# A fused attention and expert kernel: scores tied behind matmul groups, maxima in other PSUM banks, a new ration of groups a step

## The chip, the cores and the metric

The kernel runs on one core of one Trainium2 chip. The metric is the device time of one execution in microseconds (us). TensorE does the matmuls, VectorE (DVE), ScalarE (ACT) and GpSimd (POOL) the elementwise work, and SyncE (SP) issues nearly all DMAs.

## The reference

Attention with rotary positions over 4 batches, 8 heads, 576 positions and head size 64, then two expert layers on the 2304 tokens, all in f32:

```python
scores = scale * np.matmul(q_rot, k_rot.transpose(0, 1, 3, 2))
attn = np.exp(scores - np.max(scores, axis=-1, keepdims=True))
attn = attn / (np.sum(attn, axis=-1, keepdims=True) + 1e-09)
attn_out = np.matmul(attn, v)
...
x = attn_out.transpose(0, 2, 1, 3).reshape(B * S, H * D)      # 2304 x 512
h = np.maximum(np.maximum(x @ w1, x @ w2), x @ w3)            # d_ff 768
x = h @ w_out
h = x @ w_in                                                  # d_ff 2048
out = (h * (1.0 / (1.0 + np.exp(-h)))) @ w_out2
```

## The kernel before

**Tiles and steps.** Heads are taken in pairs (`hp`, 4 a batch), and a batch's 576 query rows in two parts: 256 rows (tiles 0 and 1) and 320 rows (tiles 2, 3 and 4, the last of 64 rows). That makes 80 tiles; `attention()` runs one step `j` for each and five steps more. In step j it traces the scores of tile j (`tile_scores`: one small product for the last keys, then two of 512 columns, one for each head, on 64 rows of the array each), their maximum on VectorE (`tile_max`, L436) and two Exps on ScalarE (L443); behind these come, for the tile of the step before, the division by the sum (`tile_norm`, L452 to L455) and four SP copies that move blocks of e to pt (`tile_move`, L494); for the tile two steps back, the last key column's transpose (`tile_last`, L505, L461); and for the tile three steps back the flip (`tile_flip`, L516), a transpose of 32 x 32 blocks on VectorE. When a part of a head pair is complete, `av` multiplies it with v (L557, then eight products of 64 output columns, L561) and splits the result into two f16 halves x (L564 on ScalarE, L565 on VectorE). That is the way of batches 1 to 3 (`moved(b)`); batch 0 turns all its blocks on TensorE (`tile_turn`). `qk_turn` transposes a pair's q and k (L373, L387) one pair ahead. `av_at` and `x_ready` say in which step a part's value product is traced and from which step its x may be used.

**Groups.** The first expert layer (`moe1`) is a generator of matmul groups, of which each fills one PSUM bank (L649): 12 matmuls of 256 or 320 columns for w1, w2, w3, and 18 for w_out. A group's result is emptied by ScalarE (L665) or VectorE (L667). Two banks, ring `ps_m` with the tag m, are there for groups while attention runs. After each step the main loop traces groups by a ration: `debt` grows by `RATE = 8000` columns, and each group takes off its own. A part's groups may start once `x_ready` is reached.

**PSUM.** A tile's scores take three banks and there is one such tile (`ps_s`); two banks (`ps_t`, tag tr) hold turned pieces and last columns; one (`ps_x`) the value product; two (m) the groups and, through `max_bank`, the maxima over all partitions that set the f16 scales (`all_max_a` transposes, VectorE reduces, `all_max_b` spreads; L120 and L128 on TensorE). When attention is over, its six banks are given back and five more hold groups (mg).

**Side work.** Beside all this the second layer's weights are loaded, narrowed to f16 halves and combined: L227 on ScalarE, L229 on GpSimd, L238 and L239 on VectorE (`narrow_b`), L153 on ScalarE, L917, L921 and L925 for the combinations, and about six SP transfers a step. `tc.issue_after(last["max"])` puts some of these behind the step's maximum on VectorE.

**Order.** Each engine's instructions stand in one fixed queue. A scheduler in the build makes that order from the traced program, with its own idea of durations; `with tc.issue_after(x):` forces an instruction behind x on its engine. A matmul of a later group may therefore stand ahead of, behind or between the score products of a tile.

Of the kernel before, what the change touches and what calls it, by code (L numbers as in the profile page):

```python
# [7 lines left out]
F32 = mybir.dt.float32  # L8
# [9 lines left out]
P = 128  # L18
# [4 lines left out]
def fused_kernel(  # L23
# [22 lines left out]
    nc = tc.nc  # L46
    B, H, S, D = q.shape
    NP = H // 2
# [60 lines left out]
    zscr = {nm: dram.tile([P, KC * (F2 // 512) * 512], F32, name="z" + nm) for nm in ("wi", "wo")}  # L109


    ps_am = []

    def max_bank():
        return (ps_am[0] if ps_am else ps_m).tile([P, 512], F32, tag="m", name="m")

    def all_max_a(m, ps=None):

# [240 lines left out]
    def moved(b):  # L359
        return b > 0  # L360
# [219 lines left out]
    for b, hp, r in order:  # L580
        first.setdefault((b, hp), len(tiles))
        tiles += [(b, hp, t) for t in PARTS[r][2]]
        av_at.setdefault(len(tiles) + 2 + moved(b), []).append((b, hp, r))
        x_ready[b, r] = len(tiles) + 4 + moved(b)
    for i, (b, hp) in enumerate(pairs):
        u = first[b, hp]
        if b > 1:
# [11 lines left out]
    for b in range(1, B):  # L599
# [4 lines left out]
        at(u, v_scale, b)  # L604
        at(u + 1, v_scale_b, b)

    def attention():

        back = lambda j, n: tiles[j - n] if n <= j < len(tiles) + n else None
        for j in range(len(tiles) + 5):  # L610
            if j < len(tiles):
                tile_scores(tiles[j])
                tile_max(tiles[j])
            key = back(j, 3)
            if key and moved(key[0]):
                tile_flip(key)
            for a in av_at.pop(j, ()):
                av(*a)
            key = back(j, 1)
            if key:  # L620
                tile_norm(key)
                if moved(key[0]):
                    tile_move(key)
            key = back(j, 2)
            if key:
                (tile_last if moved(key[0]) else tile_turn)(key)
            for f, a in events.pop(j, ()):
                f(*a)
            yield
# [11 lines left out]
    def group(passes, n, ps=None, more=False):  # L641

        first = ps is None
        if first:
            wide_n[0] += 1
            ring, tag = (ps_g[0], "mg") if ps_g and wide_n[0] % 7 > 1 else (ps_m, "m")
            ps = ring.tile([P, 512], F32, tag=tag, name=tag)
        for i, (l, r) in enumerate(passes):
            nc.tensor.matmul(ps[:, 0:n], l, r, start=(first and i == 0), stop=(not more and i == len(passes) - 1))  # L649
        return ps  # L650

    def moe1(b, pools):
# [632 lines left out]


    RATE = 8000
    debt = 0
    next(wprep)
    moe = wprep2 = None  # L1290
# [9 lines left out]
    for j, _ in enumerate(attention(), 1):  # L1300
        if moe is None:
            for _ in range(1 + (j > 7)):
                next(wprep, None)
            if j >= x_ready[0, 0]:
                for _ in wprep:
                    pass
                wprep2 = prep_wo1(stage2)
                moe = moe_groups()
                nxt = next(moe)
            continue  # L1310
        next(wprep2, None)
        if x_p.get(1) is not None:
            for _ in range(1 + (j % 4 == 0) if j > 20 else 0):
                next(wprep3, None)
            if hasattr(WI, "s"):
                wprep4 = wprep4 or prep_w8(1.7)
                next(wprep4, None)
        debt = min(debt + RATE, 3 * RATE)
        while debt > 0 and nxt[0] < B - 1 and j >= x_ready[nxt[0], nxt[1]]:
            debt -= nxt[2]  # L1320
            nxt = next(moe)
        if nxt[0] == B - 1 and j > len(tiles) - 4 and nxt[1] == 0:
            nxt = next(moe)
    for _ in wprep3:
        pass
    for _ in wprep4:
        pass
    attn_pools.close()
    tail = ExitStack()
    ps_g.append(Ring(tail, "ps_g", 5, space=PSUM))  # L1330
# [82 lines left out]
```

## Time and profile before

| what | value |
| --- | --- |
| time, median of 3 runs | 1001.32 us (1000.82 to 1008.92) |
| profiled execution | 1006.66 us, span 1004.8 us |
| mean granted TensorE clock | 0.969 |
| busy share PE, DVE, ACT, POOL | 92%, 70%, 60%, 49% |

The profile is of one execution, which is slower than the median of the runs. A clock of 1.0 is 2.4 GHz, 0.5 is 1.2 GHz. Shares are averages over stages with different limits: up to about 590 us attention and the first expert layer run together, to about 660 us the rest of the first expert layer, and then the second expert layer.

### The profile page before, as it was taken

How to read it: one execution, taken by the hardware profiler on the slowest of the kernel's cores; microseconds unless marked ns; L12 is line 12 of the kernel's file. 1: busy time of each engine (PE TensorE's matmuls, PEld its weight loads, DVE VectorE, ACT ScalarE, POOL GpSimd, SP SyncE). 2: the span in 40 equal slices, each digit the busy share in tenths (PEclk: the TensorE clock that was granted, in tenths of full speed). 3: DMA queues.
4: the chain of work that ended last, by engine and by line, in shares of the span. 5: the costliest groups of instructions: out<-in, count | busy, mean ns of one | idle time of the engine just before them, and what ended most of it. 6: DMA issues, size and time to landing. Idle time of an engine off the chain costs nothing. (4 is left out here: it accounts for less than half of the span.)

```text
span 1004.8 us, 19162 instructions
## 1 busy us (share of the span) xinstructions
PE 922.8 (92%) x6802; PEld 674.3 (67%) x6802; DVE 698.6 (70%) x1231; ACT 604.4 (60%) x1381; POOL 490.9 (49%) x546
## 2 busy tenths in 40 slices
PE   4577999999999899998998989999998999999997
PEld 2344665555666556665655567788887888888886
DVE  5779877967578556897767546854778767856554
ACT  2888577757667656787867623653563544554442
POOL 5835594961455500633322205653678259255264
PEclk9798999999999899999998999999999999999999
DMA  6943135877788965789988846264454253333201
GB/s 150 295 118 104 34 100 120 190 143 161 165 180 191 183 107 96 203 225 228 215 212 188 205 115 212 72 189 147 134 188 132 74 174 102 114 122 125 66 1 42
DMA packets 185198, 146.29 MB, mean 146 GB/s; under 512 B 51216, under 2 KB 168720, under 8 KB 185104
## 3 DMA queue, kind: packets, MB, share of 16 engines
q1 hardware_dynamic: 183600, 144.36, 56.5%
q8 instruction: 54, 0.88, 0.4%
q10 hardware_dynamic: 1504, 0.72, 0.3%
q14 instruction: 40, 0.33, 0.1%
HBM read 90.51 MB, written 26.21 MB: 116 GB/s over the span
## 5 line engine op out<-in xcount | busy, mean ns | idle before, releaser
L649 PEld LDWEIGHTS <-w 128*128 128x128 f16 x1632 | 161.5, 100 | 70.7 <-issue 24.5
L649 PE MATMUL m<-x,w 128*128 128x256 f16 (+1 forms) x1388 | 195.4, 292 | 13.1 <-ACT t L665 6.0
L1139 PEld LDWEIGHTS <-g 128*128 128x128 f16 x1485 | 146.2, 98 | 17.6
L1076 PEld LDWEIGHTS <-w8s 128*128 128x128 f16 x1344 | 131.1, 98 | 16.1 <-issue 1.0
L436 DVE TENSOR_REDUCE nb<-s 128x2 f32<-128x1152 f32 (+1 forms) x80 | 98.7, 1233 | 42.0 <-PE s L426 38.1
L443 ACT ACTIVATE e<-s,nb 128x576 f32<-128x576 f32 x144 | 105.3, 737 | 35.2 <-DVE nb L436 33.0
L917 POOL TENSOR_TENSOR z<-z 128x128 f32<-128x128 f32 (+1 forms) x96 | 60.8, 652 | 127.7 <-DMA z<-zwi 49.4
L229 POOL TENSOR_SCALAR z<-z 128x256 uint16<-128x256 uint16 x64 | 52.9, 826 | 123.0 <-ACT z L227 77.7
L455 ACT ACTIVATE e<-e,rec 128x576 f32<-128x576 f32 x144 | 104.5, 768 | 12.9 <-DVE rec L453 12.4
L426 PE MATMUL s<-T 64*128 64x512 f32 x256 | 85.9, 707 | 0.0
L561 PE MATMUL xp<-pt,vd 128*64 128x256 f32 (+1 forms) x512 | 81.5, 416 | 2.7 <-DVE pt L516 2.7
L1090 POOL TENSOR_TENSOR z<-t 128x256 f32<-128x256 f32 x32 | 27.1, 847 | 89.0 <-DVE t L1082 54.0
L516 DVE STREAM_TRANSPOSE pt<-pt 128x1024 f32<-128x1024 f32 (+1 forms) x60 | 67.6, 1127 | 2.8 <-DMA pt<-e 2.8
L1028 DVE SCALAR_TENSOR_TENSOR g<-gsum,sg,g 128x1024 f16<-128x1024 f32 x36 | 49.1, 1372 | 23.5 <-ACT g L1027 23.1
L352 POOL TENSOR_TENSOR w<-qk,sin_sb 128x512 f32<-128x512 f32 (+2 forms) x44 | 45.0, 1044 | 40.7 <-DMA qk<-in_q_dram 37.5
L649 PE MATMUL m<-h,wo 128*128 128x256 f16 (+1 forms) x448 | 63.2, 291 | 0.0
L1027 ACT ACTIVATE g<-gsum,sg 128x1024 f16<-128x1024 f32 x36 | 40.9, 1143 | 36.5 <-POOL gsum L1023 36.5
L649 PEld LDWEIGHTS <-wo 128*128 128x128 f16 x512 | 50.3, 100 | 17.2 <-issue 2.7
L561 PEld LDWEIGHTS xp<-pt,vd 128*64 128x64 f32 x512 | 35.9, 136 | 37.6 <-issue 13.4
L239 DVE SCALAR_TENSOR_TENSOR z<-z,z 128x256 int32<-128x256 int32 x64 | 36.3, 567 | 20.2 <-POOL z L229 19.0
L667 DVE SCALAR_TENSOR_TENSOR t<-m,t 128x256 f32<-128x256 f32 (+1 forms) x82 | 36.8, 449 | 18.5 <-PE m L649 15.7
L1139 PE MATMUL c<-w,g 128*128 128x256 f16 x376 | 48.9, 277 | 0.0
(246 smaller groups left out, 1970.7 us busy)
## 6 DMA issues: line engine op xcount, KB each, us to landing
w8s<-w8scr SPq DMA_DIRECT2D x64, 448.0 KB, 4.4
pt<-e SPq DMA_DIRECT2D x192, 128.0 KB, 4.0
z<-in_moe_w_in_dram SPq DMA_DIRECT2D x32, 256.0 KB, 3.9
z<-in_moe_w_out_dram SPq DMA_DIRECT2D x32, 256.0 KB, 3.7
w<-in_moe_w_dram SPq DMA_DIRECT2D x6, 768.0 KB, 5.2
wo<-in_moe_w_dram SPq DMA_DIRECT2D x6, 768.0 KB, 4.6
qk<-in_q_dram SPq DMA_DIRECT2D x32, 128.0 KB, 3.2
vd<-in_v_dram SPq DMA_DIRECT2D x16, 256.0 KB, 3.1
```

The lines of the kernel that those rows point to most:

```text
L229: nc.gpsimd.tensor_scalar(out=q[:, :, 2], in0=q[:, :, 1], scalar1=step, scalar2=off, op0=ALU.mult, op1=ALU.add)
L426: last["s"] = last["score"] = nc.tensor.matmul(s[:, o:o + 512], qs[r], kt[r], start=True, stop=True).ins
L436: x = nc.vector.tensor_reduce(out=nb[:, 0:m], in_=both(s, 0, 960, 576) if m > 1 else s[:, 0:576], op=ALU.max, axis=AX.X, negate=True)
L443: x = nc.scalar.activation(out=e[:, HK[g]], in_=s[:, SK[g]], func=AF.Exp, bias=nb[:, g:g + 1], accum_out=sm[:, g:g + 1])
L455: nc.scalar.activation(out=e[:, HK[g]], in_=e[:, HK[g]], func=AF.Copy, scale=r[:, g:g + 1])
L516: nc.vector.transpose(out=x, in_=x)
L561: nc.tensor.matmul(xp[r, 0:n], v4[:, g, c, :], turned(c, g), start=False, stop=(c == 3))
L649: nc.tensor.matmul(ps[:, 0:n], l, r, start=(first and i == 0), stop=(not more and i == len(passes) - 1))
L917: nc.gpsimd.tensor_tensor(out=z[:, o], in0=z[:, x], in1=z[:, y], op=op)
L1028: nc.vector.scalar_tensor_tensor(out=l, in0=x, scalar=sg_t[jb], in1=h, op0=ALU.mult, op1=ALU.subtract)
L1076: nc.tensor.matmul(o, l, r, start=(i == 0), stop=(i == len(passes) - 1))
L1139: x = nc.tensor.matmul(ps, l, r, start=first, stop=last_, skip_group_check=True)
```

## The change

Four things change. First, `max_bank` takes its bank from the turns' ring (tr) while the step's number is over `LOOSE = 25` and attention runs. Second, from the 27th tile on `tile_scores` stands inside `tc.issue_after(last["group"])`: a tile's scores come behind the last group that was traced before them. Third, for the last batch's second part, `tile_flip` comes two steps behind the tile instead of three, and `av` and `x_ready` come one step earlier. Fourth, from that tile on the ration of a step is `pace[j - 1]`: 13600 columns, less 3650 for the scores, 5800 for each value product and 2900 for each `qk_turn` of the step.

```diff
     def max_bank():
-        return (ps_am[0] if ps_am else ps_m).tile([P, 512], F32, tag="m", name="m")
+        ring, tag = (ps_am[0], "m") if ps_am else (ps_t, "tr") if b_now[0] else (ps_m, "m")
+        return ring.tile([P, 512], F32, tag=tag, name=tag)
...
-        av_at.setdefault(len(tiles) + 2 + moved(b), []).append((b, hp, r))
-        x_ready[b, r] = len(tiles) + 4 + moved(b)
+        lag = int(moved(b) and (b, r) != (B - 1, 1))
+        av_at.setdefault(len(tiles) + 2 + lag, []).append((b, hp, r))
+        x_ready[b, r] = len(tiles) + 4 + lag
...
+    LOOSE = 25
+    LAST = [(B - 1, hp, t) for hp in range(NP) for t in PARTS[1][2]]
+
     def attention():
...
+            b_now[0] = int(j > LOOSE)
             if j < len(tiles):
-                tile_scores(tiles[j])
+                with tc.issue_after(last["group"]) if j > LOOSE else nullcontext():
+                    tile_scores(tiles[j])
                 tile_max(tiles[j])
-            key = back(j, 3)
-            if key and moved(key[0]):
-                tile_flip(key)
+            for n in (3, 2):
+                key = back(j, n)
+                if key and moved(key[0]) and n == 3 - (key in LAST):
+                    tile_flip(key)
...
-            nc.tensor.matmul(ps[:, 0:n], l, r, start=(first and i == 0), stop=(not more and i == len(passes) - 1))
+            x = nc.tensor.matmul(ps[:, 0:n], l, r, start=(first and i == 0), stop=(not more and i == len(passes) - 1))
+        last["group"] = x.ins
...
+    costs = {av: 5800, qk_turn: 2900}
+    pace = [13600 - 3650 - sum(costs[f] for f, _ in jobs) for jobs in (
+        [(av, a) for a in av_at.get(j, ())] + [x for x in events.get(j, ()) if x[0] is qk_turn] for j in range(len(tiles) + 5)
+    )]
...
-        debt = min(debt + RATE, 3 * RATE)
+        debt = min(debt + (pace[j - 1] if j > LOOSE else RATE), 3 * RATE)
```

The lines of the kernel after are numbered 1 to 9 higher than those of the kernel before. On TensorE, at the 28th tile, before: the tile's scores (bank set s) with their second large product behind four groups; the "..." stands for the matmuls of four groups in banks m 1, m 0.

```order
L561 MATMUL xp_0_2236<-pt_1_1889,vd5_0_131 64x256 x8
L423 MATMUL s_0_2225<-kd3_0_125,T_3_1897 128x2x64
L426 MATMUL s_0_2225<-T_3_1897 128x512
L649 LDWEIGHTS w1_0_138
L649 MATMUL m_1_1994<-x_0_457,w1_0_138 128x320
...
L426 MATMUL s_0_2225<-T_3_1897 128x512
L505 MATMUL tr_1_2258<-ident_0_78,e_1_2081 128x128
L649 LDWEIGHTS w1f_0_137
L649 MATMUL m_1_2060<-x_0_457,w1f_0_137 128x320
```

And the same tile after:

```order
L657 MATMUL m_1_2210<-x_0_457,w1_0_138 128x320
L424 MATMUL s_0_2225<-kd3_0_125,T_3_1897 128x2x64
L427 MATMUL s_0_2225<-T_3_1897 128x512 x2
L506 MATMUL tr_1_2258<-ident_0_78,e_1_2081 128x128
L657 LDWEIGHTS w1_0_138
L657 MATMUL m_0_2281<-x_0_457,w1_0_138 128x320
```

The two large products now stand together, behind the last matmul of the group in m_1_2210, which was four groups later in the old order.

On TensorE, in the drain behind the 80th tile's scores, before: the end of one group in bank m 0 (m_0_6674), a value product (xp), and the start of the next group, again in bank m 0 (m_0_6704).

```order
L649 MATMUL m_0_6674<-x_0_5504,w1_0_138 128x256
L557 MATMUL xp_0_6646<-pt_0_6326,vd2_0_128 128x320
L505 MATMUL tr_0_6666<-ident_0_78,e_0_6544 128x128
L561 MATMUL xp_0_6646<-pt_0_6326,vd2_0_128 64x320 x8
L649 LDWEIGHTS w1_0_138
L649 MATMUL m_0_6704<-x_0_5504,w1_0_138 128x256
```

And after:

```order
L558 MATMUL xp_0_6487<-pt_0_6176,vd2_0_128 128x320
L562 MATMUL xp_0_6487<-pt_0_6176,vd2_0_128 64x320 x8
L657 LDWEIGHTS w1_0_138
L657 MATMUL m_0_6678<-x_0_5350,w1_0_138 128x256
...
L506 MATMUL tr_0_6553<-ident_0_78,e_0_6409 128x128
...
L657 MATMUL m_1_6693<-x_0_5350,w1_0_138 128x256
```

The value product comes ahead of the groups, and these alternate between the two banks m.

On VectorE, at the maximum of the 71st tile (nb), before: one flip (of tile 68) behind it, then narrowing (z), a combination (z8, w8o), evacuations (h1, t) and a reciprocal (rec), up to the 72nd tile's maximum.

```order
L436 TENSOR_REDUCE nb_2_5928<-s_0_5925 128x1
L516 STREAM_TRANSPOSE pt_1_5683<-pt_1_5683 128x1024
L238 TENSOR_SCALAR z_0_5865<-z_0_5865 128x256
L925 SCALAR_TENSOR_TENSOR z8_1_5711<-z8_1_5711,wihalf_0_4236 128x512
L674 TENSOR_TENSOR h1_7_5806<-t_3_5804,h1_7_5806 128x320
L239 SCALAR_TENSOR_TENSOR z_0_5865<-z64_0_5709,z_0_5865 128x256
L925 SCALAR_TENSOR_TENSOR w8o_0_5956<-z8_0_5788,wihalf_0_4236,w8o_0_5956 128x512
L453 RECIPROCAL rec_2_6021<-rec_2_6021 128x1
L667 SCALAR_TENSOR_TENSOR t_1_5890<-m_0_5877,t_0_5822 128x320
L436 TENSOR_REDUCE nb_3_6002<-s_0_5998 128x2
```

And after:

```order
L437 TENSOR_REDUCE nb_2_5773<-s_0_5770 128x1
L517 STREAM_TRANSPOSE pt_1_5544<-pt_1_5544 128x1024
L517 STREAM_TRANSPOSE pt_0_5723<-pt_0_5723 128x1024
L239 TENSOR_SCALAR z_0_5736<-z_0_5736 128x256
L934 SCALAR_TENSOR_TENSOR z8_1_5572<-z8_1_5572,wihalf_0_4173 128x512
L683 TENSOR_TENSOR h1_7_6005<-t_3_6003,h1_7_6005 128x320
L240 SCALAR_TENSOR_TENSOR z_0_5736<-z64_0_5570,z_0_5736 128x256
L934 SCALAR_TENSOR_TENSOR w8o_0_5802<-z8_0_5634,wihalf_0_4173,w8o_0_5802 128x512
L676 SCALAR_TENSOR_TENSOR t_1_6125<-m_0_6112,t_0_6072 128x320
L454 RECIPROCAL rec_2_5878<-rec_2_5878 128x1
L566 SCALAR_TENSOR_TENSOR x_0_5350<-xp_0_5866,vs_3_4988,x_0_5350 128x256
L437 TENSOR_REDUCE nb_3_5859<-s_0_5855 128x2
```

The flip of the 69th tile (pt_0_5723) has come up behind that of the 68th, and from here on each maximum is followed by the flip of the tile two before it.

## Rows read from the trace of the kernel before

**Rows 1.** Windows: stretch in us, length, busy us (instructions) by engine, granted clock, DMA.

```profile
187.34:576.39 389.05, 363.73 (x2305) 227.52 (x2304) 274.43 (x502) 269.84 (x749) 151.34 (x194) 0.96 0.82 181
576.39:659.65 83.26, 78.23 (x597) 58.45 (x596) 52.61 (x100) 33.92 (x65) 30.58 (x33) 0.98 0.41 124
```

**Rows 2.** Waits of TensorE, 187 to 600 us: total us, times, longest.

```profile
PE s L423 <- ACT e L443: 5.9, 6, 2.1
PE s L416 <- ACT e L443: 5.7, 2, 3.6
PE m L649 <- ACT t L665: 4.0, 5, 1.4
PE m L649 <- DVE t L667: 3.5, 1, 3.5
```

**Rows 3.** Timeline at the 73rd tile: start, us, what, [idle before <-releaser].

```profile
520.69 1.13 PE L426 MATMUL s<-T 64*128 64x512 f32 x4
...
525.55 0.43 DVE L239 SCALAR_TENSOR_TENSOR z<-z,z 128x256 int32<-128x256 int32 x1 [4.84 <-POOL z L229]
...
527.66 1.34 DVE L436 TENSOR_REDUCE nb<-s 128x2 f32<-128x1152 f32 x1
...
530.64 2.07 PE L416 MATMUL s<-T,qd 128*128 128x512 f32 x2 [3.60 <-ACT e L443]
```

**Rows 4.** Windows, as rows 1: the 28th step, and around the 74th scores.

```profile
203.38:213.13 9.75, 9.75 (x59) 6.08 (x58) 5.22 (x7) 3.58 (x10) 4.30 (x6) 1.00 0.83 144
...
526.00:540.00 14.00, 10.40 (x49) 5.99 (x49) 10.70 (x21) 10.15 (x28) 4.48 (x7) 0.76 0.87 192
```

**Rows 5.** Timeline of TensorE, the 28th and 29th tiles' scores.

```profile
203.80 1.12 PE L426 MATMUL s<-T 64*128 64x512 f32 x2
204.86 3.43 PE L649 MATMUL m<-x,w 128*128 128x320 f16 x24
208.22 1.12 PE L426 MATMUL s<-T 64*128 64x512 f32 x2
...
213.44 1.13 PE L426 MATMUL s<-T 64*128 64x512 f32 x4
```

**Rows 6.** Timeline of TensorE, two value products, the second cut.

```profile
502.60 1.95 PE L561 MATMUL xp<-pt,vd 128*64 128x256 f32 x16
...
513.96 1.51 PE L561 MATMUL xp<-pt,vd 128*64 128x256 f32 x10
...
519.20 1.08 PE L561 MATMUL xp<-pt,vd 128*64 128x256 f32 x6
```

**Rows 7.** Timeline of TensorE, the 62nd tile's scores.

```profile
445.69 0.49 PE L423 MATMUL s<-kd,T 128*128 128x128 f32 x2 [1.13 <-ACT e L443]
```

**Rows 8.** Timeline of the drain, TensorE and VectorE.

```profile
578.85 0.70 PE L557 MATMUL xp<-pt,vd 128*128 128x320 f32 x2
...
579.60 2.37 PE L561 MATMUL xp<-pt,vd 128*64 128x320 f32 x16
...
585.42 1.25 DVE L516 STREAM_TRANSPOSE pt<-pt 128x1024 f32<-128x1024 f32 x1 [2.81 <-DMA pt<-e]
...
587.11 2.23 PE L649 MATMUL m<-x,w 128*128 128x256 f16 x12 [3.50 <-DVE t L667]
...
589.72 0.70 DVE L516 STREAM_TRANSPOSE pt<-pt 128x512 f32<-128x512 f32 x1
```

**Rows 9.** Timeline, SP's copies of tiles 69 and 72, the maxima two steps on.

```profile
508.22 2.61 SPq L494 DMA_DIRECT2D pt<-e  x4
508.98 0.76 DVE L436 TENSOR_REDUCE nb<-s 128x1 f32<-128x576 f32 x1 [0.53 <-PE s L417]
...
531.35 2.65 SPq L494 DMA_DIRECT2D pt<-e  x4
...
533.07 0.76 DVE L436 TENSOR_REDUCE nb<-s 128x1 f32<-128x576 f32 x1 [0.37 <-PE s L417]
```

**Rows 10.** DMA issues: queue, count, KB each, median us to landing.

```profile
pt<-e SPq DMA_DIRECT2D x192, 128.0 KB, 4.0
```

**Rows 11.** Waits of VectorE, 187 to 600 us.

```profile
DVE z L239 <- POOL z L229: 19.0, 10, 4.8
```

More of the change, by code (lines that the diff above doesn't have):

```diff
@@ L109, in fused_kernel @@
     zscr = {nm: dram.tile([P, KC * (F2 // 512) * 512], F32, name="z" + nm) for nm in ("wi", "wo")}
-    ps_am = []
+    ps_am, b_now = [], [0]
     def max_bank():
-        return (ps_am[0] if ps_am else ps_m).tile([P, 512], F32, tag="m", name="m")
+        ring, tag = (ps_am[0], "m") if ps_am else (ps_t, "tr") if b_now[0] else (ps_m, "m")
+        return ring.tile([P, 512], F32, tag=tag, name=tag)
     def all_max_a(m, ps=None):
@@ L1327, in fused_kernel @@
         pass
+    b_now[0] = 0
     attn_pools.close()
```

## The prediction

> **What bounds the kernel now.** I began with the busy time by stretch [rows 1]. From the start of the 26th tile's scores to the start of the 80th's (187.34 to 576.39 us) the attention loop runs with the groups of the first expert layer between its steps. TensorE is busy 363.73 of 389.05 us there, so it is the bound, and it loses 25.3 us to gaps and, at a mean granted clock of 0.96, another 0.04 x 389 = 15.6 us to the lower clock. The drain behind it (to 659.65 us) loses 5.0 us to gaps and about 0.02 x 83 = 1.7 us to the clock. What lies before 187 us and after 659.65 us has the same instructions in both kernels. So 47 us is all that a pure reordering can win from waits, and what it wins beyond that must come from TensorE's own work.
>
> Next I asked what ends the gaps [rows 2]. The largest entries are scores that wait for the Exp of the tile before (5.9 + 5.7 us): the scores have one tile in PSUM, so product, maximum and Exp of a tile are a closed chain. Then come groups that wait for one of the two banks of ring m to be emptied (4.0 + 3.5 us).
>
> The longest case shows why the chain is late [rows 3]. The 73rd tile's scores end at 521.8 us, and their maximum starts only at 527.66 us: VectorE stands in its queue 4.84 us at a weight-narrowing step (L239) that wants GpSimd's half of the narrowing (L229). TensorE has two groups to do meanwhile, runs dry, and the 74th tile's scores start at 530.64 us after 3.60 us of idling; the 14 us around it have a mean granted clock of 0.76 [rows 4], that is, about half of them at 1.2 GHz instead of 2.4. The change does not touch the narrowing steps or the transfers of weights. That limits what it can win.
>
> **The change, part by part.** *Scores tied.* The tie as such removes no instruction. It fixes that a tile's scores come behind all groups traced before it. In the order, the 26th step now holds eight groups (30720 columns) where it held two, because a backlog is worked off at once; from there on each step has about two, as before. From the 27th to the 79th step the groups between two tiles' scores shrink by as much, and behind the 80th tile's scores stand 162816 columns instead of 156672: 6144 columns more, at 7680 columns in 3.36 us (204.86 to 208.22 us) [rows 5] 2.7 us of work that moves into the drain and isn't added.
>
> What the new order does remove is split pairs. The two score products of a tile use 64 rows each and run together: 1.13 us for both where they follow each other, but 1.12 us for each one where groups stand between them (213.44 against 203.80 and 208.22 us) [rows 5]. Before, five tiles are split so in the order (the 28th, 41st, 50th, 55th, 78th); after, one (the 64th). Four times 1.12 + 1.12 - 1.13 = 1.1 us is **-4.4 us** of TensorE work, in a stretch that TensorE bounds. Value products have the same trait: eight in a row take 1.95 us, while one cut into five and three takes 1.51 + 1.08 us [rows 6], 0.64 us more; part of it is pipeline fill, so I take 0.5. From the 27th step on the order has 13 such odd cuts before and 9 after: **-2 us**.
>
> *The ration.* With 13600 columns a step it aims at 5.7 us of TensorE work, value products and turned pieces included. In the order its effect is smaller than its rule: steps with a value product still have two groups, as have those without. Steps with little work are those that run dry when the chain is late. In front of two scores that waited, the 74th tile's (3.60 us, [rows 3]) and the 62nd's (1.13 us, [rows 7]), the new order has more work: three groups and part of a value product in the 73rd step instead of two groups, about 8 us against 5 with the scores. But at the 35th, 70th and 72nd steps it has less by as much. As the narrowing steps keep stalling VectorE, I take **-2 us** of gaps and clock; bounds -13 (half of what ends at an Exp, 5.8, and half of the clock's loss, 7.8) and +8 (the gaps move to steps that have become shorter).
>
> *Maxima in the turns' banks.* Four chains of an all-partition maximum leave ring m for the two banks tr. In the drain before, one such chain held bank m 1 for so long that three groups in a row had to use m 0 [rows 8]: the third waited 3.50 us for an evacuation (L667) that stood in VectorE's queue behind a flip, which stood 2.81 us for its copies, and that third group took 2.23 us, at the lower clock. After, four groups alternate between the two banks there, and the evacuation stands ahead of the flip. The last flip ended at 590.42 us, 12.8 us after the 80th scores (577.6 us), and what stands between the two in the new order (one value product at 0.70 + 2.37 us and the next one's first part at 0.70 [rows 8], five groups of 3072 columns at the pace of [rows 5], 1.34 us each, and five single transposes, at most 0.3 us each) is 12 us: about 1 us stays open. So of 6.7 us lost in the drain I take **-4 us**, bounds -6.7 and 0. A bank tr that a maximum holds is missing to the turned pieces and last columns. In the order no turned piece stands between the two products of a chain, only single last columns, so **+0.5 us**, bounds 0 and +4 (the turns wait about 1 us, as the 62nd scores did, in each chain).
>
> *The last part a step earlier.* For the last batch's second part (the 69th to 80th tiles) the flip moves from three steps behind its tile to two, and the value product, its two evacuations on ScalarE and VectorE, and the readiness of x with it. The flip needs the four copies on SP's queue, and it stands right behind a maximum, with evacuations, narrowing and reciprocals queued behind it on VectorE. By the timing of before [rows 9, 10], the 69th tile's four copies are issued from 508.22 us on, 0.65 us apart, and the fourth lands 4.0 us after its issue, at 514.2; the maximum two steps on ends at 509.7: the flip would hold VectorE 4.5 us. The same reading gives 3.5 us at the 72nd (copies from 531.35, maximum from 533.07), about 1 us each at the 70th and 75th and nothing at the six others up to the 78th: 10 us in all. What of that reaches TensorE depends on whether two groups and the pieces of a step outlast it. I take a third, **+3 us**; bounds 0 and +10. What hides the rest is the two banks of m; when an evacuation behind the flip is late, so is the third group.
>
> **The sum.** -4.4 - 2 - 2 - 4 + 0.5 + 3 = -8.9 us. It is made against the profiled execution (1006.66 us, span 1004.8); the runs' median is 1001.32, and as the terms are single stalls and instructions I carry them over unchanged: **992.5 us**. About 1% (10 us) is what a measurement of this kernel can tell from no change.
>
> **A rule weighed.** Long rows of groups through two banks are what the eight groups in the 26th step make. In the trace, four groups in a row through the same two banks (203.38 to 213.13 us) run at a granted clock of 1.00 [rows 4]. The Trainium skill, page "TensorE: Matmul & The Clock Gate", section "A second HAM failure mode: psum-queue depth-cycling", says otherwise: cycling through PSUM banks leaves TensorE tiny gaps between groups, and the clock swings between its levels. If the eight groups ran at 1.2 GHz, they would take 13.4 us more (30720 columns at 3.36 us for 7680), which gives 992.5 + 13.4 = 1006 us. By that rule the tie would cost more than it brings; the trace does not agree.
>
> **The rivals.** (a) *The chain's waits go.* If the even steps outlast VectorE's stalls, half of the 25.3 us of gaps in the loop and a third of the clock's loss go, 12.6 + 5.2 = 17.8 us in place of the 2: 1001.3 - 8.9 - 15.8 = 977 us. For it: the gaps sit at steps with two groups and nothing else. Against: the steps still hold two groups, and the stall of [rows 3] comes from transfers. (b) *The flips give the gain back.* All 10 us of flip waits reach TensorE instead of 3: 999.5 us, or 1003 with 3.4 us more lost to the clock, about what the 14 us around 530 us lost (0.24 x 14, [rows 4]). (c) *Slower: the tie holds the scores behind a blocked group.* Before, scores could pass a group whose bank is full. Now, if the evacuation of a group is queued on VectorE behind a narrowing step, the next scores wait too. VectorE's waits at L239 are 19.0 us in ten places [rows 11]; 11.6 us reach TensorE now as waits for an Exp. If all 19.0 did, the flips cost their 10 and the turns 4 us, the time is 1001.3 - 8.9 + 7.4 + 7 + 3.5 = 1010, and 1012 with as much more at the lower clock as one such case brought [rows 4]. It decides from the point where a step's groups end later than the Exp of its tile. (d) *The tie changes nothing*, since the order after the 28th step is the old one: then the split pairs and the drain alone count, and that is inside the forecast's range.
>
> **How the numbers follow.** Forecast, 984 to 1000 us: 0.55, of which 0.22 lies under 991. (a) 977: 0.20. (b) 1003: 0.13. (c) 1012: 0.09. The rule's 1006: 0.03. The range leaves out the far half of (a) and (c) each: 980 to 1006. Faster by over 1%: 0.22 + 0.20 = 0.42; slower by over 1%: 0.09; the rest, 0.49, within 1%.
>
> **What would show it.** In the profile after: score pairs of four matmuls in 1.13 us nearly everywhere; TensorE's gaps in the loop at about 23 us, still ended by Exp behind L240 (the old L239); in the drain no wait of 3.5 us for an evacuation; flips that wait for copies after the 69th tile, with a few us. Wrong would be: gaps in the loop under 12 us (then (a)), or flips that wait 10 us and groups that wait for evacuations behind them (then (b)), or scores that no longer wait for Exp while groups ahead of them wait for banks (then (c)).

## The result and the profile after

| | before | after |
| --- | --- | --- |
| time, median of the runs taken together | 1003.09 us (4 runs) | 989.89 us (4 runs, 988.1 to 995.34) |
| ratio, 95% interval | | 0.9874 [0.9842, 0.9907] |
| profiled execution | 1006.66 us, span 1004.8 us | 989.2 us, span 987.4 us |

The changed kernel is faster by 1.3%, 11.4 us under the 1001.32 us that the prediction started from; forecast were 992.5 us, 8.9 us under it. By the ratio it is 12.6 us. The profiled execution of before lies 5 us above 1001.32 us, that of after at the median of its runs, so the spans differ by 17.4 us; what follows is about these two executions.

The windows of after, for the stretches of [rows 1] (26th to 80th scores; drain, to the end of the last group) and for the rest, and last the rest of before:

```profile
186.01:562.53 376.52, 349.00 (x2282) 222.25 (x2280) 274.28 (x505) 269.08 (x749) 151.13 (x195) 0.98 0.84 187
562.53:644.20 81.67, 78.53 (x621) 59.91 (x620) 52.35 (x99) 34.81 (x66) 32.56 (x33) 1.00 0.43 128
644.20:987.40 343.20, 334.79 (x3057) 298.67 (x3055) 227.44 (x373) 168.65 (x257) 190.82 (x201) 1.00 0.37 118
```

```profile
659.65:1004.80 345.15, 336.46 (x3058) 299.56 (x3055) 226.25 (x373) 169.00 (x257) 190.48 (x201) 0.99 0.37 117
```

The loop is 12.5 us shorter. TensorE is busy 14.7 us less there and still stands 27.5 us (25.3 before): the time came out of its work and its clock (0.98 for 0.96), not out of its gaps. TensorE's waits between 187 and 600 us, to be read against [rows 2] and one more line of before:

```profile
PE m L649 <- ACT y L691: 1.2, 1, 1.2
```

```profile
PE m L657 <- ACT t L674: 7.7, 3, 4.8
PE s L424 <- ACT e L444: 6.6, 7, 1.5
PE m L657 <- DVE t L676: 5.8, 2, 3.9
PE m L657 <- ACT y L700: 4.4, 1, 4.4
PE tr L506 <- DVE kd L397: 2.5, 1, 2.5
```

The kind of wait changed and the sum hardly did. Scores that wait for an Exp fell from 11.6 to 6.8 us (0.2 us of it at L417); groups that wait for the evacuation of a bank m rose from 8.7 to 17.9 us. The tie puts the next scores behind the groups, so that a stall can meet a group first. That the tie alone does it is not shown: the longest wait of a group, at the 45th tile, is there with 3.84 and 4.37 us in the two kernels below that have the banks and no tie, too. In the changed kernel it looks like this in the timeline of GpSimd, VectorE, ScalarE and TensorE:

```profile
316.49 0.27 PE L506 MATMUL tr<-ident,e 128*128 128x128 f32 x1
316.50 2.67 POOL L926 TENSOR_TENSOR z<-z 128x128 f32<-128x128 f32 x6 [4.93 <-DMA z<-zwi]
320.04 0.43 DVE L240 SCALAR_TENSOR_TENSOR z<-z,z 128x256 int32<-128x256 int32 x1 [4.19 <-POOL z L230]
320.56 0.42 ACT L154 ACTIVATE junk<-z 128x256 bf16<-128x256 f32 x1 [3.23 <-DVE z L240]
321.09 0.44 ACT L674 ACTIVATE t<-m 128x320 f32<-128x320 f32 x1
321.58 1.33 PE L657 MATMUL m<-x,w 128*128 128x320 f16 x5 [4.82 <-ACT t L674]
```

It is read upwards. TensorE waits for ScalarE's evacuation, which stands in the queue behind the bound of a narrowed weight (L154); that waits for VectorE's L240, that for GpSimd's half L230, and L230 stands behind six sums (L926) that waited 4.93 us for weights from a DMA. It is the stall of [rows 3] at another place. In the drain, where [rows 8] had a wait of 3.50 us:

```profile
571.25 1.25 DVE L517 STREAM_TRANSPOSE pt<-pt 128x1024 f32<-128x1024 f32 x1 [2.19 <-DMA pt<-e]
572.94 1.47 PE L657 MATMUL m<-x,w 128*128 128x256 f16 x12 [1.90 <-DVE t L676]
```

A flip still waits for its copies and a group behind it for an evacuation, but 1.90 us, and the group takes 1.47 us instead of 2.23.

To see where the 15.4 us until the end of the last group went (659.65 to 644.2 us), the trace was split. Each matmul counts from its start to the start of the next, or to its end if that is sooner; half of what ran at the lower clock is put under "clock"; what is left is work at full clock; time without a matmul is "gaps". The same for every kernel of this study, in us, with two counts from the order of TensorE's instructions: score pairs that are split, and value products cut after an odd number of their eight matmuls.

| kernel | pairs split | odd cuts | score work | value work | all work | gaps | clock | end | ratio of times |
| --- | --- | --- | --- | --- | --- | --- | --- | --- | --- |
| before | 5 | 18 | 116.2 | 95.5 | 561.1 | 73.3 | 25.2 | 659.7 | 1 |
| after | 1 | 14 | 111.1 | 92.8 | 552.1 | 71.4 | 20.7 | 644.2 | 0.9874 |
| e1_no_tie | 4 | 15 | 113.8 | 93.2 | 555.2 | 76.1 | 25.5 | 656.8 | 0.9971 |
| e2_no_early | 1 | 16 | 111.0 | 94.0 | 553.4 | 71.2 | 20.9 | 645.5 | 0.9882 |
| e3_no_bank | 1 | 11 | 110.4 | 90.7 | 549.4 | 82.6 | 24.3 | 656.4 | 0.9969 |
| e4_no_ration | 0 | 11 | 110.7 | 90.7 | 551.6 | 77.8 | 15.3 | 644.8 | 0.9888 |
| f1_split_all | 64 | 14 | 186.7 | 93.4 | 631.8 | 38.1 | 21.9 | 691.8 | 1.0318 |
| f2_tie_bank | 0 | 12 | 111.9 | 91.3 | 554.7 | 74.0 | 17.7 | 646.3 | 0.9897 |
| f3_loose24 | 0 | 12 | 109.0 | 91.2 | 547.7 | 77.8 | 23.5 | 648.9 | 0.9917 |
| f4_tie_only | 0 | 12 | 110.6 | 91.1 | 552.9 | 82.7 | 21.9 | 657.5 | 0.9973 |
| g1_bank_only | 3 | 16 | 115.3 | 93.9 | 559.0 | 68.4 | 20.8 | 648.2 | 0.9934 |
| g2_half_bank | 1 | 13 | 110.6 | 92.3 | 551.0 | 80.2 | 23.4 | 654.7 | 0.9965 |
| g3_narrow_act | 1 | 12 | 112.0 | 91.5 | 554.0 | 71.6 | 12.0 | 637.6 | 0.9824 |
| g4_before_rate | 3 | 13 | 112.5 | 91.7 | 552.0 | 71.0 | 23.3 | 646.2 | 0.9881 |

Before to after: work -9.0 (scores -5.1, values -2.7, the rest -1.2), gaps -1.9, clock -4.5. Part of that is chance. Ahead of the 26th tile's scores the order of TensorE's 849 matmuls is the same in both kernels, and work differs by -1.9 us there, gaps by -2.2 and clock by +2.9. What the change can have done lies behind: work -7.1 (scores -3.9, values -2.9), gaps +0.3, clock -7.4. Behind the last group the instructions are the same again, and 1.7 of the 2.0 us less there are one half-speed stretch of 3.4 us that this execution did not have.

The table has one execution of each kernel. Ten of them (all but f1, f3, g3 and g4) share the order ahead of the 26th tile's scores, and still have 131.5 to 136.8 us of work there, 38.4 to 44.0 of gaps and 7.1 to 15.1 of clock. Differences of that size between two rows need no cause. All runs list their span and mean granted clock, though. The span times what the mean clock lacks to 1, below called the clock's share of the span (low clock in gaps counts in it), is 27.1 to 29.1 us in before and 24.0 in after; the remaining span is 973 and 965.0 us.

### The profile page after: what moved, and what is told of

Its sections match the earlier page's. It is cut to its first block, busy times and chain, and to the rows that moved or that the text cites. A ratio compares the mean times of both kernels' runs of the same rounds, so it can differ in the third digit from the quotient of the medians.

```text
span 987.4 us, 19157 instructions
## 1 busy us (share of the span) xinstructions
PE 907.6 (92%) x6802; PEld 669.8 (68%) x6802; DVE 700.4 (71%) x1231; ACT 604.0 (61%) x1381; POOL 492.2 (50%) x546
## 5 line engine op out<-in xcount | busy, mean ns | idle before, releaser
L657 PE MATMUL m<-x,w 128*128 128x256 f16 (+1 forms) x1356 | 190.8, 291 | 18.5 <-ACT t L674 10.0
L437 DVE TENSOR_REDUCE nb<-s 128x2 f32<-128x1152 f32 (+1 forms) x80 | 98.5, 1232 | 35.2 <-PE s L427 27.1
L926 POOL TENSOR_TENSOR z<-z 128x128 f32<-128x128 f32 (+1 forms) x96 | 62.4, 668 | 121.9 <-DMA z<-zwi 71.9
L230 POOL TENSOR_SCALAR z<-z 128x256 uint16<-128x256 uint16 x64 | 51.9, 810 | 107.8 <-ACT z L228 80.6
L562 PE MATMUL xp<-pt,vd 128*64 128x256 f32 (+1 forms) x512 | 79.4, 416 | 0.9 <-DVE pt L517 0.9
L427 PE MATMUL s<-T 64*128 64x512 f32 x256 | 78.6, 684 | 0.0
L1099 POOL TENSOR_TENSOR z<-t 128x256 f32<-128x256 f32 x32 | 27.1, 846 | 87.3 <-DVE t L1091 52.2
L562 PEld LDWEIGHTS xp<-pt,vd 128*64 128x64 f32 x512 | 35.5, 137 | 36.8 <-issue 14.7
L240 DVE SCALAR_TENSOR_TENSOR z<-z,z 128x256 int32<-128x256 int32 x64 | 36.8, 575 | 19.2 <-POOL z L230 18.2
L1148 PE MATMUL b<-w,g 128*128 128x256 f16 x376 | 48.5, 273 | 0.0
L1148 PE MATMUL a<-w,g 128*128 128x256 f16 x376 | 47.9, 273 | 0.0
```

Of the source, the lines that this page charges most:

```text
L230: nc.gpsimd.tensor_scalar(out=q[:, :, 2], in0=q[:, :, 1], scalar1=step, scalar2=off, op0=ALU.mult, op1=ALU.add)
L427: last["s"] = last["score"] = nc.tensor.matmul(s[:, o:o + 512], qs[r], kt[r], start=True, stop=True).ins
L437: x = nc.vector.tensor_reduce(out=nb[:, 0:m], in_=both(s, 0, 960, 576) if m > 1 else s[:, 0:576], op=ALU.max, axis=AX.X, negate=True)
L562: nc.tensor.matmul(xp[r, 0:n], v4[:, g, c, :], turned(c, g), start=False, stop=(c == 3))
L657: x = nc.tensor.matmul(ps[:, 0:n], l, r, start=(first and i == 0), stop=(not more and i == len(passes) - 1))
L926: nc.gpsimd.tensor_tensor(out=z[:, o], in0=z[:, x], in1=z[:, y], op=op)
```

## The experiments

The theories at the start were these. Theory 1 is the prediction's: work that is no longer cut, and the drain. Theory 2: the ration's even steps. A third: the last part a step earlier. The first four kernels are the changed kernel minus one part each.

**The tie undone** (e1_no_tie):

```diff
-                with tc.issue_after(last["group"]) if j > LOOSE else nullcontext():
+                with nullcontext():
                     tile_scores(tiles[j])
```

> The kernel after without the tie; banks, ration and early last part stay. In its order four of the five split score pairs are back (after: one) and one odd cut more of a value product. Theory 1 (the gain is TensorE work that is no longer cut, plus the drain): 3 x 1.1 + 0.5 = 3.8 us lost, 994 us. Theory 2 (the gain is the even steps that the ration makes, so that fewer waits for an Exp are left): the ration stays, no loss, 990 us within 1.5.

Measured 1000.9 us, 0.9971 [0.995, 0.9993]: about 10 us of the gain are gone. In the table, work +3.1, gaps +4.7, clock +4.8. One gap of 7.39 us, at the 61st tile, is not in the changed kernel. Its timeline:

```profile
434.56 0.42 DVE L240 SCALAR_TENSOR_TENSOR z<-z,z 128x256 int32<-128x256 int32 x1 [3.11 <-POOL z L230]
...
435.69 1.34 DVE L437 TENSOR_REDUCE nb<-s 128x2 f32<-128x1152 f32 x1
...
439.49 0.72 ACT L930 ACTIVATE w8o<-z,wihalf 128x512 f16<-128x512 f32 x1 [3.90 <-DMA w8scr<-w8o]
...
440.96 0.74 ACT L444 ACTIVATE e<-s,nb 128x576 f32<-128x576 f32 x1
...
442.57 0.80 PE L424 MATMUL s<-kd,T 128*128 128x128 f32 x2 [7.39 <-ACT e L444]
```

The step has two groups, and no maximum over all partitions holds a bank m in it. The Exp is late because VectorE waits 3.11 us at a narrowing step ahead of the tile's maximum, and ScalarE another 3.90 us for a DMA at a combination of weights (L930) that stands ahead of the Exp.

**The last part not earlier** (e2_no_early):

```diff
-        lag = int(moved(b) and (b, r) != (B - 1, 1))
+        lag = int(moved(b))
...
-    LAST = [(B - 1, hp, t) for hp in range(NP) for t in PARTS[1][2]]
+    LAST = []
```

> The kernel after with the flips three steps behind and the value product of the last part where it was. Theory 1: the early flips cost VectorE some waits, of which I forecast 3 us for TensorE, so 987 us; if the two banks m hide them, 990 us. Theory 3 (the early last part shortens the drain, and that is the gain there): 3 to 4 us slower, 994 us.

Measured 990.53 us, 0.9882 [0.9861, 0.9903], the same as with it. VectorE's flips wait 3.1 us for copies (187 to 600 us) instead of 9.7, and TensorE's gaps are 71.2 instead of 71.4 us: the 6.6 us do not show on the path. The edit takes back the earlier flips and the earlier value product together, so the worth of each alone is open.

**The maxima back in ring m** (e3_no_bank):

```diff
-            b_now[0] = int(j > LOOSE)
+            b_now[0] = 0
```

> The kernel after with the maxima in ring m again. Its order has the same single split pair and three odd cuts fewer. Theory 1: the drain has one bank for its groups again and waits about 3.5 us with the clock lowered behind it, +4 us, less 1.5 us for the cuts: 992.5 us. Theory 2: no change, 990 us. If the banks tr had been the bottleneck of the turns (the price that I put at 0.5 us, bound 4): 987 us.

Measured 1000.44 us, 0.9969 [0.9947, 0.9992]: again 10 us, and these are gaps (+11.2). The timeline at the 41st tile shows them:

```profile
289.68 0.27 PE L121 MATMUL m<-ident,vm 128*1 128x128 f32 x1
...
289.90 0.93 PE L657 MATMUL m<-x,w 128*128 128x256 f16 x7
...
297.82 0.27 DVE L123 TENSOR_REDUCE amax<-m 1x1 f32<-1x128 f32 x1
297.93 0.79 PE L424 MATMUL s<-kd,T 128*128 128x128 f32 x2 [7.11 <-DVE z L239]
```

The maximum's transpose takes a bank m at 289.68 us, and VectorE, stalled at its narrowing steps, reads it only at 297.82 us. For 8 us there is one bank for groups, and the order has given this step one group; TensorE runs dry for 7.11 us. The 61st tile has the same with 8.70 us. In the changed kernel the bank is one of tr and both steps have two groups. The held bank is not the whole cause: one group more is 1.34 us of work at the pace of [rows 5], and e1_no_tie and f3_loose24, with their maxima in tr and two groups in the step, stand 7.39 and 7.41 us at the 61st tile as well. The long part is the late Exp. At the 80th tile's scores this kernel is only 1.9 us behind the changed one; the groups that it left undone make its drain 92.0 us long instead of 81.7.

**The ration undone** (e4_no_ration):

```diff
-        debt = min(debt + (pace[j - 1] if j > LOOSE else RATE), 3 * RATE)
+        debt = min(debt + RATE, 3 * RATE)
```

> The kernel after with the old ration of 8000 columns a step; tie, banks and early last part stay. Its order has no split pair and three odd cuts fewer than after, and 150528 columns behind the last scores instead of 162816. Theory 1: 990 - 1.1 - 1.5 = 987.5 us. Theory 2 (the ration's even steps make the gain): steps with a value product and two groups are long again, the others short: +6 us, 996 us.

Measured 992.0 us, 0.9888 [0.9865, 0.9911]. The interval overlaps that of after; the medians differ by 2.1 us. Behind that small sum stand two larger terms of opposite sign. From the 26th tile's scores on, this execution has 3.8 us less work than after, most of it by its fewer cuts, and 4.7 us more in gaps and clock.

Losing 10 us with either of two parts is more than theory 1 prices, and theory 2 falls as the account of the whole gain. By the runs' spans and granted clocks, both losses come with a lower clock: its share of the span is 32.5 us in the 12 runs of e1_no_tie and 32.4 in those of e3_no_bank, against 24.0 in after, and the remaining span is 966.1 and 965.6 us, against 965.0. Part of this share lies in the gaps themselves (9.0, 8.6 and 4.9 us in the profiled executions), so gaps and clock are no separate causes here. The next theory was that the gain is of the tie and the banks together, neither being worth much alone. A rival stood beside it: that the accidents of one order against another are as large. The price of a split pair was measured by itself.

**Every score pair split** (f1_split_all): the small score product is issued between the two large ones.

```diff
-        nc.tensor.matmul(both(s, 512, 448, 64), qs, K, start=True, stop=True)
...
-            last["s"] = last["score"] = nc.tensor.matmul(s[:, o:o + 512], qs[r], kt[r], start=True, stop=True).ins
+            x = nc.tensor.matmul(s[:, o:o + 512], qs[r], kt[r], start=True, stop=True).ins
+            if g == 0:
+                with tc.issue_after(x):
+                    y = nc.tensor.matmul(both(s, 512, 448, 64), qs, K, start=True, stop=True).ins
+            last["s"] = last["score"] = x
```

> The changed kernel, but with the scores' small 64-row-shared product placed between the two large ones, so that every tile's pair of large products is cut apart; the arithmetic is the same. Theory 1 (the prediction's price): a pair takes 1.12 + 1.12 us instead of 1.13, that is 1.1 us more for each tile; in the attention loop alone 55 tiles, where TensorE is the bound, so 55 to 65 us more than the changed kernel: 1045 to 1055 us. Rival: the price of a cut pair is mostly pipeline fill that the next matmul takes up, so that under 15 us are lost: 992 to 1005 us.

Measured 1035.77 us, 1.0318 [1.0272, 1.0365]. The groups of TensorE's instructions give the large score products 157.3 us, against 78.6 in the changed kernel:

```profile
L426 PE MATMUL s<-T 64*128 64x512 f32 x256 | 157.3, 697 | 5.4 <-ACT e L447 4.9 <-ACT T L380 0.3
```

```profile
L427 PE MATMUL s<-T 64*128 64x512 f32 x256 | 78.6, 684 | 0.0
```

The price of the prediction holds, and more: 75.6 us of score work for 63 more pairs are 1.2 us each. But the last group ends only 47.6 us later: TensorE's gaps fell by 33.3 us. In the loop's window TensorE stands 8.9 us of 398 and the mean clock is 1.00:

```profile
211.90:610.17 398.27, 389.33 (x2281) 230.94 (x2280) 268.35 (x503) 270.64 (x748) 148.71 (x191) 1.00 0.79 175
```

So work added to TensorE here is paid to about 60% (47.6 of 79.7), and the rest fills time in which it would have waited. In the loop alone it is less than half: 46.0 us of work made it 22 us longer (398.27 against 376.52 us). That work taken away comes back in part as gaps is likely by this, but no run here shows it by itself.

**Tie and banks alone** (f2_tie_bank): the changed kernel with the edits of e2_no_early and e4_no_ration together.

> The changed kernel without its ration (8000 columns a step as before) and without the last part a step earlier: tie and banks alone. Theory of tie and banks together (they are the whole gain, since each alone left about 2.5 us): 990 to 993 us. Theory 1 (work that is no longer cut: 0 split pairs and 12 odd value cuts in the order, against 1 and 14 in the changed kernel, but no even steps): 988 to 990 us. Rival that the time follows the order's accidents: anywhere from 988 to 1001.

Measured 992.15 us, 0.9897 [0.9868, 0.9926]: the whole gain within the intervals. Against e2_no_early it lacks the ration alone, and the two terms of e4_no_ration are there again: from the 26th tile's scores on, work is 3.3 us lower, and gaps and clock are 6.3 us higher.

**From a tile earlier** (f3_loose24):

```diff
-    LOOSE = 25
+    LOOSE = 24
```

> The changed kernel with tie, ration and banks from the 26th tile on instead of the 27th: the order of everything behind it is shifted by a step, and the row of eight groups at the 26th step is gone. Theory of tie and banks together: the gain doesn't depend on the place, 989 to 993 us. Rival (accidents of the order decide, the tie and the banks being good for nothing by themselves): somewhere between 989 and 1001, with other gaps at other steps.

Measured 994.4 us, 0.9917 [0.9886, 0.9949], just past the range of the theory. It has the least work of all kernels here (547.7 us) and loses that to gaps (77.8) and clock: TensorE stands 7.41 us at the 61st tile, behind the same two waits as in e1_no_tie, and 3.13 us at the 41st, where the transpose of a maximum waits for a bank tr.

**The tie alone** (f4_tie_only): f2_tie_bank with the edit of e3_no_bank.

> The kernel before with the tie alone (no ration, maxima in ring m, no earlier last part). Theory of tie and banks together: the tie without the banks is worth little, 999 to 1002 us, with gaps of 4 us and more where a maximum holds one of the two banks m across the next scores. Theory 1: 0 split pairs and 12 odd cuts instead of 5 and 18, 994 to 996 us. Rival that the tie is the gain: 990 us.

Measured 998.87 us, 0.9973 [0.9953, 0.9994]. Work is 8.2 us under that of before, and gaps are 9.4 us over it: the tie takes the cuts away and pays for it in gaps. Held banks are part of it: groups wait 3.08 and 1.90 us for VectorE's reading of a maximum (L123).

**The banks alone** (g1_bank_only): f2_tie_bank with the edit of e1_no_tie.

> The kernel before with the maxima in the turns' banks from the 27th tile on, and nothing else of the change. Theory of tie and banks together: alone the banks are worth little, 998 to 1002 us. Theory that the banks are the gain by themselves: 990 to 993 us. Theory 1 (cut work and the drain's one bank): 3 split pairs instead of 5 and 4 us of the drain, 994 to 997 us.

Measured 996.17 us, 0.9934 [0.991, 0.9957], under the theory's 998 and in the range of theory 1. The banks bring something without the tie, too. Against before, work is 2.1 us less, gaps 4.9 and clock 4.4; but 4.5 of the gaps' 4.9 us lie ahead of the 26th tile's scores, where the order is the same. Behind it the differences are -3.7, -0.4 and -6.9 us.

**The banks in the first half** (g2_half_bank):

```diff
-            b_now[0] = int(j > LOOSE)
+            b_now[0] = int(LOOSE < j < 47)
```

> The changed kernel, but with the maxima in the turns' banks only up to the 47th tile; from there on they are in ring m, as before. Theory (a maximum in bank m holds the bank until VectorE reads it, and the step has one group only): no long gap at the 41st tile, where the kernel without any such banks lost 7.1 us, but one of 7 to 9 us at the 61st tile, where that kernel lost 8.7 us; half of the loss comes back: 993 to 997 us. Rival (the order's accidents elsewhere): no gap at the 61st tile, and the time is 990, or 1000 with gaps at other tiles.

The gaps came out at the places expected. At the 41st tile the gap is 1.83 us; at the 61st, where the maximum is in ring m again, the timeline shows the row of e3_no_bank once more:

```profile
424.96 0.27 PE L121 MATMUL m<-ident,vm 128*1 128x128 f32 x1
...
432.77 0.27 DVE L123 TENSOR_REDUCE amax<-m 1x1 f32<-1x128 f32 x1
...
434.71 0.80 PE L424 MATMUL s<-kd,T 128*128 128x128 f32 x2 [8.06 <-ACT e L444]
```

There the changed kernel has a value product and two groups in front of the next scores, and no gap:

```profile
425.22 2.37 PE L562 MATMUL xp<-pt,vd 128*64 128x320 f32 x14
...
428.34 2.24 PE L657 MATMUL m<-x,w 128*128 128x256 f16 x19
...
430.51 0.49 PE L424 MATMUL s<-kd,T 128*128 128x128 f32 x2
```

The time did not: 999.66 us, 0.9965 [0.9945, 0.9984], as slow as with no bank at all. The gap saved at the 41st tile is found again at the 45th (4.62 us, against 2.09 in e3_no_bank at the 46th); at the 61st tile both kernels have the same lead over before (15.5 and 15.6 us), and both lose it there and behind. In the changed kernel the Exp of the 61st tile starts at 428.93 us, in this one at 433.12 us: VectorE waits 4.04 us at L240 ahead of the maximum here, and not there. So a gap that is gone at one place can come back at another, and the gap at the 61st tile is again a late Exp more than a missing group.

**Before, with 8100 columns a step** (g4_before_rate):

```diff
-    RATE = 8000
+    RATE = 8100
```

> The kernel before with 8100 instead of 8000 columns a step, which reshuffles the order of the whole loop and changes nothing else (3 split pairs and 13 odd value cuts in the order instead of 5 and 18). If the order's accidents are worth about as much as the change, it comes out anywhere from 990 to 1010 us. If tie and banks are the gain, it stays within 4 us of before, 997 to 1003 us. By theory 1's prices it should be 4 us faster, 997 us.

Measured 991.06 us, 0.9881 [0.986, 0.9902]. The theory of tie and banks as the gain falls with this run: one number that does little but reshuffle the order is worth as much as the whole change. It has 9.1 us less work than before, like the changed kernel, and about its gaps. Over its four runs the clock's share of the span is 27.9 us, as in before (28.0), so that its gain lies in work and gaps (961.3 against 973.2 us). Its gap of 6.97 us at the 61st tile does not keep it from that.

**The narrowing's second half on ScalarE** (g3_narrow_act):

```diff
-                    W.narrow_a(n - 2, part.get(n - 2), pool=True)
+                    W.narrow_a(n - 2, part.get(n - 2))
```

> The changed kernel, but with the second half of each narrowing step of the large weights on ScalarE instead of GpSimd, so that VectorE's next step no longer waits behind GpSimd's other work. Theory (what is left of the gaps comes through GpSimd's queue): VectorE's 18 us of waits go, TensorE's gaps in the loop fall by 10 us or more, 975 to 983 us. Rival (60 steps of some 0.43 us more on ScalarE, 26 us, delay the Exp as much): 988 to 998 us.

Measured 985.06 us, 0.9824 [0.98, 0.9848]: the fastest kernel here, between the two expectations. Neither account fits. TensorE's gaps between the 27th and the 80th scores are as in the changed kernel (24.8 us against 24.9), but the longest in the loop is 2.85 us instead of 4.82, and the clock's loss there 1.7 instead of 7.4 us. The five runs agree in this: the clock's share of the span is 20.1 us, against 24.0 in after, and the remaining span 963.6 against 965.0 us. That the shorter longest gap is what spared the clock is argued, not shown. VectorE's waits at L240 for GpSimd are gone; it waits 19.8 us for ScalarE's sums of the Exp (L453) instead, since each moved instruction takes ScalarE not 0.43 but 0.78 us. The group of ScalarE's instructions in the loop:

```profile
L232 ACT ACTIVATE z<-z 128x256 uint16<-128x256 uint16 x61 | 46.4, 778 | 0.0
```

## Why the prediction was right, and where not

**Split pairs, -4.4.** Right. Score work fell by 5.1 us for four pairs fewer, 3.9 of them from the 26th tile's scores on. For that part a straight line through the 13 kernels other than f1_split_all gives 1.12 us a pair (correlation 0.99), where the step took 1.1.

**Odd cuts, -2.** Right, and a little small: 2.7 us for four cuts. The same line for value work gives 0.68 us a cut (correlation 0.99); [rows 6] said 0.64, and the 0.5 taken from it for a supposed pipeline fill was no improvement.

**That the loop is bounded by TensorE**, so that each us of its work is a us of time, is true to less than half for work that is added there (f1_split_all). This is why a gain in work of 7 to 9 us does not fix the time to better than the gaps: apart from f1_split_all these range from 68 to 83 us in kernels with nearly the same instructions.

**Gaps and clock in the loop, -2.** Mis-sized, within its bounds of -13 and +8. From the 27th to the 80th scores gaps went from 23.3 to 24.9 us and the clock's loss from 13.1 to 7.4: -4.1 us, all of it clock. The reason given, even steps by the ration, fits: in the two pairs of kernels that differ in the ration alone, gaps and clock from the 26th tile's scores on are 4.7 and 6.3 us lower with it (one execution each). What the step missed is the price: the ration's orders have more cuts, 3.8 and 3.3 us of work, so that little time is left of it: 2.1 and 1.6 us between medians, within the intervals.

**The drain, -4.** Right: gaps 5.0 to 3.1 us, clock 1.7 to 0, together -3.6, with 2.0 us more work beside it, where the 6144 columns were put at 2.7.

**Maxima in tr, +0.5.** No wait of a turned piece for such a maximum is in the list of waits. In f3_loose24 one maximum's transpose waits 3.13 us for such a bank. What the step missed is the other side: with the tie, kernels that keep the maxima in ring m have more gaps. The three kernels with the tie and ring m for all or half of the maxima have 80.2 to 82.7 us; the five with the tie and the banks and no other edit of the work 71.2 to 77.8; the four without the tie 68.4 to 76.1. The prediction put the banks' worth in the drain alone. How the banks do it is shown in part only: held banks are the wait itself in f4_tie_only (5.0 us), but the long gaps of the other two are late Exps, as two kernels with the banks have them, too.

**The flips, +3.** Their waits for copies grew by 6.9 us on VectorE (2.8 to 9.7), against 10 forecast, and nothing of it shows in the time (e2_no_early, whose edit also takes the earlier value product back). Rival (b) did not come.

**The rivals.** (a), 977 us: not so; the gaps stayed. (c), 1012 us, was half right as a mechanism: scores wait less for an Exp and groups more for banks, as it said, but as the same stall met at another instruction, not as a further one. With the maxima in ring m the tie comes close to costing what it saves (f4_tie_only, 0.9973), though no more. The rule weighed, 1006 us, did not come: the window around the eight groups of the 26th step has a granted clock of 1.00. The Trainium skill, page "TensorE: Matmul & The Clock Gate", section "A second HAM failure mode: psum-queue depth-cycling", tells of a bf16 kernel, at 512 columns a matmul, whose clock swung while it cycled through PSUM banks. Carried over to these groups it would swing here; the trace does not show it.

```profile
186.00:204.00 18.00, 15.42 (x108) 10.43 (x107) 11.60 (x24) 9.50 (x27) 17.51 (x19) 1.00 0.95 206
```

**As a whole** the sum of -8.9 stands against -11.4 us of the medians (-12.6 by the ratio): right in size, with the work term confirmed by its own price (-6.4 against -7.1 from the 26th tile's scores on), and the clock term too small. Some of it is luck: the sum takes a us of work for a us of time, which f1_split_all does not bear out, and nothing in it foresaw that undoing the tie or the banks costs 10 us each. What the prediction never asked is whether the order of before was a typical one. It has the most split pairs and odd cuts of all kernels but f1_split_all, and g4_before_rate loses most of them by a change of 1% in a rate. The tie holds the split pairs at 0 or 1 in every order tried; the five kernels with tie and banks are at 0.987 to 0.992, the four without the tie at 0.988 to 1. That the tie makes the gain surer is suggested by that, not shown: two rates without the tie are too few. Also open is what sets the clock's loss: between the 27th and the 80th scores it is 13.1 us in before, 7.4 in after and 5.3 in g4_before_rate, with gaps of 23.3, 24.9 and 24.1 us.

## What to carry to other kernels

Before a change of order is credited with its time, run the old kernel with one harmless number changed: here that alone was worth 12.6 of 1003.67 us. Two matmuls that share the array by rows are to be kept next to each other; count the cut pairs in the instruction order, since one price (1.1 us a score pair, 0.7 us an odd cut of a value product) fits all kernels here. When an order is tied down, look for what takes a bank of the tied groups and is read late by a busy engine, and try it in a bank of another ring. Long stalls are worth breaking up even where their sum stays: moving 61 small instructions off a queue that waits for DMAs came with a shorter longest gap and a higher clock. And read a trace's account beside a stretch in which nothing changed: it shows how much two executions differ by chance.

## What the runs showed of the hardware

The six gaps of 6.9 us and more in these kernels (e1, e3 twice, f3, g2, g4) each had a stretch of 6.8 or 10.2 us at 1.2 GHz that began in the gap and outlasted it. The one of e1_no_tie, whose gap ended at 442.57 us:

```profile
438.00:448.00 10.00, 5.43 (x19) 2.98 (x20) 6.06 (x13) 6.26 (x18) 2.51 (x5) 0.52 0.82 245
```

Of shorter gaps the length does not tell by itself whether the clock falls. In g3_narrow_act TensorE stood 2.85 us before 336.12 us, and the window around it stays at 1.00; a gap of 2.32 us at 314 us in the same execution lies in a window of 0.88:

```profile
330.00:345.00 15.00, 12.15 (x84) 7.63 (x85) 7.89 (x11) 8.98 (x24) 5.20 (x6) 1.00 1.14 225
312.00:326.00 14.00, 11.68 (x71) 6.88 (x72) 6.84 (x15) 10.49 (x30) 4.64 (x8) 0.88 0.96 188
```

On ScalarE the copy of every fourth 16-bit number (L232, 256 a partition) takes 778 ns, where the one that reads every second 32-bit number and writes 256 of them (L228) takes 436 ns; GpSimd took 813 ns for the former in the changed kernel.
